# The last six units' second product: two token tiles by seven half-size products, and the order around it

## Chip, core and metric

The kernel runs on one core of a Trainium2 chip. The metric is the device time of one execution in microseconds (us); lower is better.

## What is computed

```python
def sm_attn(qq, kk, vv):
    s = scale * np.matmul(qq, kk.transpose(0, 1, 3, 2))
    a = np.exp(s - np.max(s, axis=-1, keepdims=True))
    a = a / (np.sum(a, axis=-1, keepdims=True) + 1e-09)
    return np.matmul(a, vv)
p_packed = sm_attn(p, k, v)            # p: (8, 8, 32, 64); k, v: (8, 8, 576, 64)
out = sm_attn(q, p_packed, p_packed)   # q: (8, 8, 576, 64)
x = out.transpose(0, 2, 1, 3).reshape(4608, 512)
xn = x / rms(x) * rms_g
return (silu(xn @ w_gate) * (xn @ w_val)) @ w_out    # 512 -> 1536 -> 512
```

8 batches of 8 heads, 576 tokens each, 32 packed rows per head. The three weights arrive as float64, all else as float32.

## The kernel before

**Products.** Since the second attention's output is a weighted sum of 32 packed rows, the kernel never forms x: it multiplies the packed rows of a batch into the gate and value weights once (packed weights, `packed_weights`: six chunks `c` of 256 columns for each of gate and value, kept in `ring`), and the attention weights `aTu` of the tokens are then the moving operand of the **first product** (line 1439). A float32 product is done in three float16 passes, high by high, high by low and low by high; each operand is therefore split into a high half (a cast) and a low half (a subtraction).

**Units.** The 4608 tokens are 12 units of 384, each three token tiles of 128. Units 1, 4, 7 and 10 hold tokens of two batches (192 columns of each). `mlp` runs the units: for each of 12 pieces `ft` of the hidden width six matmuls for gate and six for value (line 1439) into two PSUM rooms `pm`; `gated` makes silu(gate) * value (ScalarE, line 1520, and VectorE, line 1523), casts the high half into `hall` (ScalarE, line 1542) and subtracts for the low half (GpSimd, line 1545, or VectorE, line 1548). Then the **second product**: for each of three token tiles 12 x 3 matmuls of 512 columns (line 1506) into one PSUM room, from `hall` as the stationary operand and the split w_out, `wo`, as the moving one; in the last unit the third tile is done in two halves of 256 columns (line 1480). `store` evicts with the scale `invE` and sends the tile out.

**The start.** The gate and value weights arrive as 8-byte numbers in 12 pieces of 1 MB (`gv_piece`); `to_f32` makes float32 of the two words of each, with one conversion of a piece's low words on ScalarE (line 396) or GpSimd (line 391) or none but VectorE steps, as the string `LOW` says. For each chunk a Gram matrix of its columns (line 447), its largest entry (line 452) and a few one-column steps (lines 340 to 345, 460 to 467) give the powers of two by which the chunk is scaled. Packed weights of batches 0 to 2 use float32; from batch 3 on (`PW16_FROM`) a float16 copy, `wgv16`, made by `weights16` (lines 1072, 1074) in the same SBUF.

**Packed rows.** The first attention's values of a batch are made in two halves of heads, `pk`, by float32 matmuls (line 887), or, for batch 7 (`V16_FROM`), by float16 ones (line 809); each half is turned by a 64-row matmul (line 919).

**Order.** Every engine runs its instructions in order, and so does the queue of SyncE (SP), which issues nearly all transfers: loads, transposes (`DMA_TRANSPOSE`) and stores. The order comes from a list: each part of the kernel is a generator that asks for a PSUM or SBUF room (`Room`), for a mark of another part, or for an engine step, and `ORDER` names, step by step, which generator goes next. `FILLS` puts matmuls without a use (line 1603) at places of the start.

## Time and profile before

| | |
|---|---|
| time of three runs, us | 729.67 median (728.51 to 732.56) |
| the profiled execution, us | 728.67, its span 726.8 |
| TensorE busy | 708.9 us (98%), 8153 matmuls |
| VectorE, ScalarE, GpSimd busy | 465.2, 476.5, 213.4 us |
| chain of work that ended last | TensorE 83%, ScalarE 5%, DMA 4% |
| DMA | 86.73 MB moved, mean 119 GB/s |

The span runs from the first to the last instruction; the profiled execution's time is 1.9 us longer. Busy times of the engines overlap, so they don't add up; the chain is the sequence of steps in which each one waited for the one ahead of it.

### The profile page before, as it was taken

Reading aid. Unit: us, or ns where it says so; the run is one execution under the profiler, and the core shown is the slowest. Engines: PE = TensorE matmul, PEld = TensorE weight load, DVE = VectorE, ACT = ScalarE, POOL = GpSimd, SP = SyncE. Lnnn points to the kernel's source line nnn. Section 1 sums busy time; section 2 is a strip of 40 time slices with the busy share of each in tenths; the row PEclk is TensorE's granted clock in tenths of the full one; section 3 lists DMA queues with packets and bytes.
Section 4 is the critical chain, followed back from the end, with each engine's and each line's share of the span. In section 5 each row is a group of like instructions: output and inputs, shape, how many; then the busy total and the mean of one; then the engine's idle time right before and its main releaser. Section 6 shows DMA issues by size and latency. Waiting matters only on the chain.

```text
span 726.8 us, 19520 instructions
## 1 busy us (share of the span) xinstructions
PE 708.9 (98%) x8153; PEld 431.8 (59%) x8153; DVE 465.2 (64%) x1032; ACT 476.5 (66%) x982; POOL 213.4 (29%) x228
## 2 busy tenths in 40 slices
...
PEclk9999999999999999999999999999999999999999
...
GB/s 286 368 371 290 199 2 74 88 158 190 55 142 120 126 99 138 168 75 136 79 209 98 77 153 161 51 115 126 132 38 24 96 82 80 51 3 51 15 2 44
DMA packets 152923, 86.73 MB, mean 119 GB/s; under 512 B 116737, under 2 KB 140161, under 8 KB 152834
## 3 DMA queue, kind: packets, MB, share of 16 engines
...
q8 instruction: 64, 1.05, 0.6%
...
## 4 chain that ended last, share of the span: by engine, by line
PE 83%; ACT 5%; DMA 4%; SPq 3%; DVE 2%; issue 1%; POOL 1%; ACTq 0%; POOLq 0%; DVEq 0%
PE pm_2x L1439 10%; PE pm_0x L1506 10%; PE pm_1x L1439 9%; PE pm_3x L1439 9%; PE pm_1x L1506 9%; PE pm_3x L1506 9%; PE pm_0x L1439 8%; PE pm_2x L1506 5%; DMA hall<-in_moe_w_val_dram 2%; SPq L423 2%; PE psa L1238 2%; PE psb L887 1%; PE pm_1x L1052 1%; PE psa L756 1%; PE pm_0x L1052 1%
## 5 line engine op out<-in xcount | busy, mean ns | idle before, releaser
L1439 PEld LDWEIGHTS <-ring 128*128 128x128 f16 x2304 | 205.1, 98 | 83.8 <-issue 10.7
L1506 PEld LDWEIGHTS <-hall 128*128 128x128 f16 x1188 | 113.3, 98 | 137.1 <-issue 6.7
L1545 POOL TENSOR_TENSOR hall<-t_1x,hall 128x384 f16<-128x384 f32 x68 | 65.0, 956 | 229.9 <-ACT hall L1542 221.7
L1545 POOL TENSOR_TENSOR hall<-t_0x,hall 128x384 f16<-128x384 f32 x60 | 58.7, 978 | 124.0 <-ACT hall L1542 115.1
L1506 PE MATMUL pm_1x<-wo,hall 128*128 128x512 f16 x360 | 80.8, 379 | 1.3 <-issue 0.7
L1506 PE MATMUL pm_3x<-wo,hall 128*128 128x512 f16 x324 | 73.2, 379 | 0.0
L1506 PE MATMUL pm_0x<-wo,hall 128*128 128x512 f16 x324 | 72.6, 379 | 0.0
L1542 ACT CAST hall<-t_1x 128x384 f16<-128x384 f32 x69 | 35.0, 507 | 17.5 <-DVE t_1x L1523 17.3
L1439 PE MATMUL pm_2x<-aTu_0x,ring 128*128 128x384 f16 (+1 forms) x318 | 45.7, 287 | 0.0
L1542 ACT CAST hall<-t_0x 128x384 f16<-128x384 f32 x70 | 35.5, 507 | 15.1 <-DVE t_0x L1523 15.0
L1439 PE MATMUL pm_1x<-aTu_1x,ring 128*128 128x192 f16 (+1 forms) x318 | 44.7, 284 | 0.0
L1439 PE MATMUL pm_2x<-aTu_1x,ring 128*128 128x192 f16 (+1 forms) x324 | 44.7, 282 | 0.0
L1439 PE MATMUL pm_3x<-aTu_0x,ring 128*128 128x192 f16 (+1 forms) x306 | 42.4, 282 | 0.0
L1506 PE MATMUL pm_2x<-wo,hall 128*128 128x512 f16 x180 | 40.0, 379 | 0.0
L1439 PE MATMUL pm_3x<-aTu_1x,ring 128*128 128x192 f16 (+1 forms) x270 | 38.9, 287 | 0.2 <-ACT t_1x L1520 0.2
L1439 PE MATMUL pm_1x<-aTu_0x,ring 128*128 128x384 f16 (+1 forms) x246 | 38.8, 299 | 0.1
L1439 PE MATMUL pm_0x<-aTu_0x,ring 128*128 128x192 f16 (+1 forms) x282 | 38.0, 279 | 0.7 <-issue 0.7
L1439 PE MATMUL pm_0x<-aTu_1x,ring 128*128 128x384 f16 (+1 forms) x240 | 36.5, 294 | 0.0
L1074 POOL TENSOR_TENSOR wgv<-o_1x,wgv 128x512 f16<-128x512 f32 x20 | 23.4, 1172 | 41.3 <-ACT wgv L1072 41.1
L1520 ACT ACT_TABLE_LOAD x15 | 19.2, 1283 | 7.3 <-PE pm_1x L1439 2.4
L1520 ACT ACTIVATE t_0x<-pm_0x,usc_1x 128x384 f32<-128x384 f32 x13 | 7.5, 577 | 22.3 <-PE pm_0x L1439 21.6
L354 DVE SCALAR_TENSOR_TENSOR ring<-pm_1x,ring 128x512 f16<-128x512 f32 x17 | 11.7, 685 | 14.7 <-ACT ring L352 14.6
...
## 6 DMA issues: line engine op xcount, KB each, us to landing
...
hall<-in_moe_w_out_dram SPq DMA_DIRECT2D x4, 1024.0 KB, 6.1
...
wo<-in_moe_w_gate_dram SPq DMA_DIRECT2D x3, 1024.0 KB, 16.0
wo<-in_moe_w_val_dram SPq DMA_DIRECT2D x3, 1024.0 KB, 14.5
...
```

Of the source, the lines that this page charges most:

```text
L354: nc.vector.scalar_tensor_tensor(lo, x, s, hi, ALU.mult, ALU.subtract)
L423: nc.sync.dma_start(raw.rearrange("p k n e -> p k (n e)"), (w_gate, w_val)[n][:, 4 * c * P : 4 * (c + 1) * P].rearrange("(kt p) f -> p kt ...
L756: nc.tensor.matmul(psc[32 * j : 32 * j + 32, hf, : HC * CP], pT[:, 2 * g + hl, 32 * j : 32 * j + 32], kT[:, j * NCK + HC * hf : j * NCK + ...
L887: nc.tensor.matmul(pp[32 * j : 32 * j + 32, :D], a1T[:, c, 32 * j : 32 * j + 32], vf[:, j, cv, :], start=(c == 0), stop=(c == NCK - 1),)
L1052: nc.tensor.matmul(ps[e][32 * j : 32 * j + 32, :], pg[h, lp, j, :], wgv16[h, c, j, lw, :], start=(n3 == 0), stop=(n3 == 2),)
L1074: nc.gpsimd.tensor_tensor(wgv16[:, c, k, 1], st, wgv16[:, c, k, 0], ALU.subtract)
L1238: nc.tensor.matmul(ps2[o : o + n, i, :, pi, :], qT[:, lq, i, pi, o : o + n], packs[b][3][:, lp, pi, :, :], start=(j == 0), stop=(j == 2),)
L1439: nc.tensor.matmul(psi[:, :, o : o + n], pw[:, g, lw, w, f * P : (f + 1) * P], aT[:, :, la, g, o : o + n], start=(j == 0), stop=(j == 5),)
L1506: nc.tensor.matmul(po, hall[:, ft, lh, ts], wo[:, ft, 1 - lw, :], start=(n == 0), stop=(n == 3 * NFT - 1))
L1520: nc.scalar.activation(t, pss[0][:, :UT], AF.Silu, scale=sc[:, c, 0:1])
L1542: nc.scalar.copy(hall[:, ft, 0, :], t)
L1545: nc.gpsimd.tensor_tensor(hall[:, ft, 1, :], t, hall[:, ft, 0, :], ALU.subtract)
```

## The change

- **Units 6 to 11** (`STR_FROM`): tile 2 is done as before (line 1593 after the change). Tiles 0 and 1 are taken together with the two halves of the hidden width of each chunk and the two halves of the output as a 2 x 2 block product, done with seven products in place of eight: `seven`, 7 x 18 matmuls of 256 columns (line 1724). The sums of the four blocks of the left operand are made per chunk in `parts_of` (line 1678), by GpSimd for chunks 0, 2, 4 and VectorE for 1, 3, 5, then split (lines 1690); those of w_out once in `tees`; `together` adds the products from PSUM (line 1739).
- **Room** for these operands is what `wgv16` held: the float16 weights are written to DRAM (line 1165) and come back, 1 MB per chunk and batch, for batches 4 to 7 (`stream`, line 1105). Batch 7's values take the float32 path (`V16_FROM`).
- **Start**: `gram` is a part of its own and accumulates both column halves of a chunk in one place, so its reduction is 256 wide; some of its small steps and five byte conversions go to GpSimd.
- **Packed weights**: odd chunks from batch 2 on take the PSUM room `psc` in place of two `pm`. **Packed rows** of both halves of heads are turned by one matmul of 128 rows.
- A new `ORDER`, new `FILLS`, and scales that follow from the above.

```diff
-LOW = "DDPAAAPAPAPP"
+LOW = "DDPPPPPPPPPP"
...
-V16_FROM = 7
+V16_FROM = 8
+STREAM_FROM = 4
+STR_FROM = 6
+TEE_BY = "PPPPPP"
+SUM_BY = "PDPDPD"
+SLO_BY = "PPPPPP"
 KEYS_GATE = 'scored'
-PW_WIDE = 8
+PAIR_FROM = 2
...
+    dram = ctx.enter_context(tc.tile_pool(name="dram", bufs=1, space=bass.MemoryType.DRAM))
+    wdram = [dram.tile([P, NKT, 2, 512], F16, name=f"wdram{c}") for c in range(NFC)]
...
-        if n == 0:
-            return
-        yield ("w32", i - 1)
+    def gram(c):
         xb = wgv[:, c].bitcast(BF16)[..., 1::2]
+        yield ("w32", 2 * c)
         pn = yield Room("pa")
-        yield PE, pe(128, 16) + 0.24, plan.now, 1.0, 32
         for w in range(2):
-            for f in range(2):
-                for kt in range(NKT):
-                    r = xb[:, kt, w, f * P : (f + 1) * P]
-                    nc.tensor.matmul(
-                        pn[:, (2 * w + f) * P : (2 * w + f + 1) * P], r, r, start=(kt == 0), stop=(kt == NKT - 1)
-                    )
+            if w:
+                yield ("w32", 2 * c + 1)
+            yield PE, pe(128, 8) + 0.03, plan.now, 1.0, 16
+            for k in range(2 * NKT):
+                f, kt = divmod(k, NKT)
+                r = xb[:, kt, w, f * P : (f + 1) * P]
+                nc.tensor.matmul(pn[:, w * P : (w + 1) * P], r, r, start=(k == 0), stop=(k == 2 * NKT - 1))
         mx = tiny(2)
-        yield DVE, dve(512) + 0.04
-        nc.vector.tensor_reduce(mx, pn.rearrange("p (w f) -> p w f", w=2), AX.X, ALU.max)
+        yield DVE, dve(256) + 0.04
+        nc.vector.tensor_reduce(mx, pn[:, : 2 * P].rearrange("p (w f) -> p w f", w=2), AX.X, ALU.max)
         yield PE, pe(2, 2)
         nc.tensor.matmul(pn[:, 0:2], margin, upper(mx), start=True, stop=True)
+        u, s = tiny(2), gv_r[:, c]
+        yield DVE, 0.37
+        nc.vector.tensor_scalar(
+            u.bitcast(U32), pn[:, 0:2].bitcast(U32), 24, 23, ALU.logical_shift_right, ALU.logical_shift_left
+        )
+        nc.vector.tensor_single_scalar(s.bitcast(U32), u.bitcast(U32), EXP_MASK, ALU.bitwise_xor)
+        plan.give("pa", pn)
         yield "g",
-        yield DVE2, 0.82
-        u, s = tiny(2), gv_r[:, c]
-        norm_scale(u, s, pn[:, 0:2])
-        plan.give("pa", pn)
-        nc.vector.tensor_scalar(ratio[:, c : c + 1], u[:, 0:1], s[:, 1:2], 0.5, ALU.mult, ALU.mult)
-        t0 = plan.now
+        yield POOLS, 1.05
+        nc.gpsimd.tensor_scalar(u, u, 2.0**-126, 2.0**51, ALU.max, ALU.mult)
+        nc.gpsimd.tensor_scalar(s, s, 2.0**127, 2.0**-51, ALU.min, ALU.mult)
+        nc.gpsimd.tensor_scalar(ratio[:, c : c + 1], u[:, 0:1], s[:, 1:2], 0.5, ALU.mult, ALU.mult)
         plan.mark("pw_sc", c)
-        by = nc.gpsimd if GV_BY[c] == "P" else nc.vector
-        yield (POOLS, 2.0, t0) if GV_BY[c] == "P" else (DVE, 0.45, t0)
-        by.tensor_scalar(gv_sc[:, c, 0:1], u[:, 0:1], gmax, 2.0**-5, ALU.mult, ALU.mult)
-        by.tensor_scalar(gv_sc[:, c, 1:2], s[:, 0:1], gmax_r, 2.0**-12, ALU.mult, ALU.mult)
-        by.tensor_scalar(wo_sc[:, c : c + 1], u[:, 0:1], u[:, 1:2], gsq, ALU.mult, ALU.mult)
-        if H32:
-            by.tensor_scalar(gv_sc[:, c, 2:3], gv_sc[:, c, 1:2], wo_sc[:, c : c + 1], 2.0**-8, ALU.mult, ALU.mult)
+        yield POOLS, 1.05
+        nc.gpsimd.tensor_scalar(gv_sc[:, c, 0:1], u[:, 0:1], gmax, 2.0**-5, ALU.mult, ALU.mult)
+        nc.gpsimd.tensor_scalar(gv_sc[:, c, 1:2], s[:, 0:1], gmax_r, 2.0**-5, ALU.mult, ALU.mult)
+        nc.gpsimd.tensor_scalar(wo_sc[:, c : c + 1], u[:, 0:1], u[:, 1:2], gsq, ALU.mult, ALU.mult)
...
-        yield PE, pe(128, 8), t_p, 1.0, 8
-        for g in range(2):
-            nc.tensor.matmul(pt[64 * g : 64 * g + 64, : 4 * NPK], pks[g], ident32, start=True, stop=True)
+        yield PE, pe(128, 4), t_p, 1.0, 4
+        nc.tensor.matmul(pt[:, : 4 * NPK], pkp[0].rearrange("p g d -> p (g d)"), ident32, start=True, stop=True)
...
-            if b < PW_WIDE:
+            if b < PAIR_FROM or c % 2 == 0:
...
+            if b >= STREAM_FROM:
+                yield ("ws", b, c)
+                w16 = streamed.pop((b, c))
...
+    def stream():
+        for b in range(STREAM_FROM, B):
+            for c in range(NFC):
+                w16 = yield Room("wst")
+                yield ("dw", c)
+                yield LOAD, P * 8192
+                nc.sync.dma_start(w16, wdram[c])
+                streamed[b, c] = w16
+                plan.mark("ws", b, c)
...
+    def tees(i):
+        for c in range(2 + i // 2, NFC, NFC):
+            yield ("dw", c)
+            yield ("pwd", c)
+        yield ("wo_hl", i)
+        if i == 0:
+            a = yield Room("a1")
+            for k in range(2):
+                plan.give("t", a[:, UT * k : UT * (k + 1)])
+        o1 = yield Room("o")
+        o2 = yield Room("o")
+        by = nc.gpsimd if TEE_BY[i] == "P" else nc.vector
+        kind = (lambda n: (POOL, pool(n))) if TEE_BY[i] == "P" else (lambda n: (DVE2, dve(n)))
+        q = DM // 2
+        for x, f in ((o1, 2 * i), (o2, 2 * i + 1)):
+            yield kind(512)
+            by.tensor_tensor(x, wo[:, f, 1, :], wo[:, f, 0, :], ALU.add)
+        for a, b, d in ((o1[:, q:], o1[:, :q], o1[:, :q]), (o2[:, q:], o1[:, q:], o1[:, q:]), (o2[:, q:], o1[:, :q], o2[:, q:]), (o2[:, :q], o2[:, q:], o2[:, :q])):
+            yield kind(256)
+            by.tensor_tensor(d, a, b, ALU.subtract)
+        t0 = plan.now
+        for w, x in enumerate((o1, o2)):
+            yield ACT, act(512), t0
+            nc.scalar.copy(teev[:, i, w, 0], x)
+            yield DVE2, dve(512) + 0.08
+            nc.vector.tensor_tensor(teev[:, i, w, 1], x, teev[:, i, w, 0], ALU.subtract)
+            plan.give("o", x)
+        plan.mark("tee", i)
...
+            if k == NKT - 1:
+                yield LOAD, P * 8192
+                nc.sync.dma_start(wdram[c], wgv16[:, c])
+                plan.mark("dw", c)
...
-            for i in range(2 if u == 0 else 0, TPU):
+            for i in (2,) if u == 0 or u >= STR_FROM else range(TPU):
...
+            if u >= STR_FROM:
+                plan.add(together(u), "store", u, 0)
+                yield from seven(u)
...
+    def parts_of(u, ft, t, sc):
+        c, f = divmod(ft, 2)
+        x3 = t.rearrange("p (i n) -> p i n", i=TPU)
+        h3 = hall[:, ft].rearrange("p l (i n) -> p l i n", i=TPU)
+        own = slice(0, TPU) if f else slice(0, TPU, 2)
+        n = UT if f else 2 * P
+        yield ACT, act(n)
+        nc.scalar.copy(h3[:, 0, own], x3[:, own])
+        if (H_LO_MIXED if len(parts(u)) > 1 else H_LO_ONE)[ft] == "P":
+            yield POOL, pool(n)
+            nc.gpsimd.tensor_tensor(h3[:, 1, own], x3[:, own], h3[:, 0, own], ALU.subtract)
+        else:
+            yield DVE2, dve(n) + 0.08
+            nc.vector.tensor_tensor(h3[:, 1, own], x3[:, own], h3[:, 0, own], ALU.subtract)
+        plan.mark("h", u, ft)
+        if ft == NFT - 1:
+            plan.give("usc", sc)
+        if f == 0:
+            evens[c] = t
+            plan.mark("even", u, c)
+            return
+        yield ("even", u, c)
+        te = evens.pop(c)
+        a11, a21 = te[:, :P], te[:, P : 2 * P]
+        a12, a22 = t[:, :P], t[:, P : 2 * P]
+        x0 = yield Room("o")
+        x = x0.rearrange("p (k n) -> p k n", k=4)
+        by = nc.gpsimd if SUM_BY[c] == "P" else nc.vector
+        kind = (POOL, pool(P)) if SUM_BY[c] == "P" else (DVE2, dve(P))
+        for d, a, b, op in ((x[:, 0], a21, a22, ALU.add), (x[:, 1], x[:, 0], a11, ALU.subtract), (x[:, 2], a11, a21, ALU.subtract), (x[:, 3], a12, x[:, 1], ALU.subtract)):
+            yield kind
+            by.tensor_tensor(d, a, b, op)
+        t0 = plan.now
+        plan.give("t", te)
+        plan.give("t", t)
+        s12r = s12[:, c].rearrange("p l (k n) -> p l k n", k=2)
+        ends = []
+        for d, r in ((s12r, slice(0, 2)), (hall[:, 2 * c, :, P : 2 * P].unsqueeze(2), slice(2, 3)), (s4[:, c].unsqueeze(2), slice(3, 4))):
+            n = P * (r.stop - r.start)
+            yield ACT, act(n), t0
+            nc.scalar.copy(d[:, 0], x[:, r])
+            if SLO_BY[c] == "P":
+                yield POOL, pool(n)
+                nc.gpsimd.tensor_tensor(d[:, 1], x[:, r], d[:, 0], ALU.subtract)
+            else:
+                yield DVE2, dve(n) + 0.08
+                nc.vector.tensor_tensor(d[:, 1], x[:, r], d[:, 0], ALU.subtract)
+            ends.append(plan.now)
+        plan.now = max(ends)
+        plan.give("o", x0)
+        plan.mark("s", u, c)
...
+    def seven(u):
+        q = DM // 2
+        tile0, tile1 = slice(0, P), slice(P, 2 * P)
+        A = {
+            1: lambda c, l: hall[:, 2 * c, l, tile0], 2: lambda c, l: hall[:, 2 * c + 1, l, tile0],
+            3: lambda c, l: s4[:, c, l, :], 4: lambda c, l: hall[:, 2 * c + 1, l, tile1],
+            5: lambda c, l: s12[:, c, l, :P], 6: lambda c, l: s12[:, c, l, P:],
+            7: lambda c, l: hall[:, 2 * c, l, tile1],
+        }
+        w = lambda f, l, h: wo[:, f, 1 - l, q * h : q * (h + 1)]
+        W = {
+            1: lambda c, l: w(2 * c, l, 0), 2: lambda c, l: w(2 * c + 1, l, 0), 3: lambda c, l: w(2 * c + 1, l, 1),
+            4: lambda c, l: teev[:, c, 1, l, :q], 5: lambda c, l: teev[:, c, 0, l, :q],
+            6: lambda c, l: teev[:, c, 1, l, q:], 7: lambda c, l: teev[:, c, 0, l, q:],
+        }
+        for k in (1, 6, 7, 5, 2, 4, 3):
+            ps = yield Room("pm")
+            for c in range(NFC):
+                if c % 2 == 0:
+                    for d in (c, c + 1):
+                        yield ("h", u, 2 * d + 1)
+                        if k not in (1, 2, 4):
+                            yield ("s", u, d)
+                        yield ("tee", d)
+                    yield PE, pe(q, 6) + 0.006, None, 1.0, 12
+                for n3, (la, lw) in enumerate(((0, 0), (0, 1), (1, 0))):
+                    nc.tensor.matmul(
+                        ps[:, :q], A[k](c, la), W[k](c, lw), start=(c + n3 == 0), stop=(c == NFC - 1 and n3 == 2)
+                    )
+            products[u, k] = ps
+            plan.mark("p", u, k)
...
+    def together(u):
+        q = DM // 2
+        o1 = yield Room("o")
+        o2 = yield Room("o")
+        def take(k):
+            yield ("p", u, k)
+            return products.pop((u, k))
+        def add(d, ps, x):
+            yield DVE, dve(q) + 0.06
+            nc.vector.scalar_tensor_tensor(d, ps[:, :q], invE, x, ALU.mult, ALU.add)
+        dst = out[u * UT : (u + 1) * UT, :].rearrange("(p c) n -> c p n", c=TPU)
+        ps = yield from take(1)
+        yield ACT, act(q)
+        nc.scalar.activation(o1[:, :q], ps[:, :q], AF.Copy, scale=invE)
+        plan.give("pm", ps)
+        ps = yield from take(6)
+        yield from add(o2[:, q:], ps, o1[:, :q])
+        plan.give("pm", ps)
+        ps = yield from take(7)
+        yield from add(o2[:, :q], ps, o2[:, q:])
+        plan.give("pm", ps)
...
```

**VectorE in the start**, around one chunk's norm: `tensor_reduce` is the reduction of the Gram matrix, `tiny` and `gv_r` hold the powers of two, line 354 is the low half in an eviction of packed weights, line 413 a step of the weights' conversion to float32. Before:

```order
L452 TENSOR_REDUCE tiny_15x<-pm_1x 128x2
L354 SCALAR_TENSOR_TENSOR ring<-pm_0x,gv_r,ring 128x512
L340 TENSOR_SCALAR tiny_17x<-pm_1x 128x2
L344 TENSOR_SCALAR tiny_17x<-tiny_17x 128x2
L345 TENSOR_SCALAR gv_r<-tiny_17x 128x2
L460 TENSOR_SCALAR ratio<-tiny_17x,gv_r 128x1
L452 TENSOR_REDUCE tiny_16x<-pm_2x 128x2
L354 SCALAR_TENSOR_TENSOR ring<-pm_3x,gv_r,ring 128x512
```

After:

```order
L413 SCALAR_TENSOR_TENSOR wgv<-wgv,wo_78 128x4x256
L471 TENSOR_REDUCE tiny_13x<-pm_1x 128x2
L1215 TENSOR_SCALAR aT_0x<-psb 128x256
L476 TENSOR_SCALAR tiny_14x<-pm_1x 128x2
L479 TENSOR_SCALAR gv_r<-tiny_14x 128x2
L1009 SCALAR_TENSOR_TENSOR pg_0x<-pts_0x,sv_269,gcol 128x128
L471 TENSOR_REDUCE tiny_15x<-pm_3x 128x2
```

The reduction is followed by two small steps in place of four; the other evictions and steps between them are others now.

**GpSimd at the end of the last unit.** Before, one low half after another (`t_0x`, `t_1x` hold silu(gate) * value):

```order
L1545 TENSOR_TENSOR hall<-t_1x,hall 128x384
L1545 TENSOR_TENSOR hall<-t_0x,hall 128x384
L1545 TENSOR_TENSOR hall<-t_1x,hall 128x384
L1545 TENSOR_TENSOR hall<-t_0x,hall 128x384
L1545 TENSOR_TENSOR hall<-t_1x,hall 128x384
```

After, from the end of chunk 4 on (`wgv` and `misc` are the memory that now holds the sums' splits; line 1657 is the low half of line 1545, 2x128 where two of the three tiles need one):

```order
L1678 TENSOR_TENSOR wgv<-t_1x 128x128
L1678 TENSOR_TENSOR wgv<-t_0x,wgv 128x128
L1690 TENSOR_TENSOR wgv<-o_1x,wgv 128x256
L1657 TENSOR_TENSOR hall<-a_0x,hall 128x384
L1690 TENSOR_TENSOR wgv<-wgv 128x256
L1690 TENSOR_TENSOR hall<-o_1x,hall 128x128
L1690 TENSOR_TENSOR hall<-wgv,hall 128x128
L1690 TENSOR_TENSOR wgv<-o_0x,wgv 128x256
L1690 TENSOR_TENSOR misc<-o_1x,misc 128x128
L1690 TENSOR_TENSOR hall<-o_0x,hall 128x128
L1690 TENSOR_TENSOR misc<-wgv,misc 128x128
L1690 TENSOR_TENSOR misc<-o_0x,misc 128x128
```

Two sums of chunk 4 and its splits (256, 128, 128 columns), and those of chunk 5, stand among the low halves; chunk 5's sums are VectorE's.

**SyncE from the transposes of unit 8 to those of unit 9** (`aTu`). Before:

```order
L1396 DMA_TRANSPOSE aTu_0x<-hl_0x 128x12x128
L1206 DMA_TRANSPOSE big_3x<-big_4x 128x24x128
L1580 DMA out_dram<-o_1x 128x512
L799 DMA_TRANSPOSE a1T_0x<-hl_0x 128x12x128
L1156 DMA big_1x<-in_q_dram 64x8x192 x2
L1580 DMA out_dram<-o_0x 128x512
L1275 DMA_TRANSPOSE aT_0x<-hl_0x 128x12x128
L1580 DMA out_dram<-o_1x 128x512
L799 DMA_TRANSPOSE a1T_0x<-hl_0x 128x12x128
L1396 DMA_TRANSPOSE aTu_1x<-hl_0x 128x12x128
```

After, the last twelve rows up to the same place:

```order
L1765 DMA out_dram<-o_0x 128x512
L1775 DMA out_dram<-wgv 128x512
L570 DMA big_3x<-in_v_dram 96x4x384
L1804 DMA out_dram<-o_1x 128x512
L1105 DMA wgv<-wdram_134 128x4096
L1365 DMA_TRANSPOSE aT_0x<-hl_0x 128x12x128
L1105 DMA wgv<-wdram_135 128x4096
L1105 DMA wgv<-wdram_136 128x4096
L1246 DMA big_1x<-in_q_dram 64x8x192 x2
L880 DMA_TRANSPOSE a_1x<-hl_0x 128x12x128
L1105 DMA wgv<-wdram_131 128x4096
L1485 DMA_TRANSPOSE aTu_1x<-hl_0x 128x12x128
```

Reloads from `wdram` stand between stores, the transposes of `aT` and `a` and the load of q, ahead of the transpose of `aTu`.

## Rows read from the trace of the kernel before

**Rows 1.** The page: parts 1 and 2 (busy time; granted clock in 40 slices).

```profile
PE 708.9 (98%) x8153; PEld 431.8 (59%) x8153; DVE 465.2 (64%) x1032; ACT 476.5 (66%) x982; POOL 213.4 (29%) x228
PEclk9999999999999999999999999999999999999999
```

**Rows 2.** Windows: length, busy PE, PEld, DVE, ACT, POOL (count), clock, DMA share, GB/s.

```profile
0.00:58.79 58.79, 49.37 (x733) 37.73 (x734) 43.92 (x98) 40.85 (x71) 22.72 (x39) 1.00 1.02 347
20.00:40.00 20.00, 15.77 (x251) 13.12 (x250) 16.94 (x34) 14.65 (x22) 5.62 (x5) 1.00 1.05 384
40.00:60.00 20.00, 16.56 (x301) 12.07 (x289) 19.46 (x43) 19.48 (x39) 11.94 (x16) 1.00 1.05 379
160.00:180.00 20.00, 18.69 (x219) 9.01 (x219) 12.84 (x38) 12.79 (x31) 4.67 (x4) 1.00 0.87 177
220.00:240.00 20.00, 18.71 (x247) 8.84 (x246) 15.69 (x46) 10.69 (x25) 7.99 (x7) 1.00 0.71 128
483.00:543.00 60.00, 60.00 (x673) 35.30 (x671) 40.38 (x82) 42.34 (x86) 12.70 (x14) 1.00 0.52 115
```

**Rows 3.** The chain that ended last, from 690: start, length, what.

```profile
690.21 0.97 PE pm_2x L1439 x6
699.96 7.77 PE pm_0x L1506 x36
719.43 3.94 PE pm_3x L1480 x36
```

**Rows 4.** The same chain in mixed unit 1.

```profile
124.82 0.99 PE pm_2x L1439 x12
```

**Rows 5.** The page, part 5: two groups, busy us, mean ns of one.

```profile
L1439 PEld LDWEIGHTS <-ring 128*128 128x128 f16 x2304 | 205.1, 98 | 83.8 <-issue 10.7
L1545 POOL TENSOR_TENSOR hall<-t_1x,hall 128x384 f16<-128x384 f32 x68 | 65.0, 956 | 229.9 <-ACT hall L1542 221.7
```

**Rows 6.** Line 1545 on POOL: min/median/max ns; then who waited.

```profile
L1545 POOL TENSOR_TENSOR hall<-t_1x,hall x68: 904/914/1462, 67.1 to 701.7; 128x384 f16<-128x384 f32 x68
L1545 POOL TENSOR_TENSOR hall<-t_0x,hall x60: 910/914/1832, 69.5 to 699.4; 128x384 f16<-128x384 f32 x60
  ACT t_1x L1520: 4.3, 9
```

**Rows 7.** Other sizes on POOL, one on DVE (groups by shape); line 391.

```profile
L1074 POOL TENSOR_TENSOR wgv<-o_1x,wgv 128x512 f16<-128x512 f32 x20 | 23.4, 1172 | 41.3 <-ACT wgv L1072 41.1
L1023 POOL TENSOR_SCALAR pgh_0x<-pg_0x,ratio 128x128 f32<-128x128 f32 x2 | 1.2, 610 | 1.0 <-DVE ratio L460 1.0
L1023 DVE TENSOR_SCALAR pgh_0x<-pg_0x,ratio 128x128 f32<-128x128 f32 x2 | 0.6, 286 | 0.1
...
L391 POOL TENSOR_SCALAR hall<-hall x4: 1127/1440/1822, 40.5 to 75.8; 128x1024 uint32<-128x1024 uint8 x4
```

**Rows 8.** The start: lines 452 and 396, DVE groups before 62, the timeline at 57.

```profile
L452 DVE TENSOR_REDUCE tiny_15x<-pm_1x x1: 680/680/680, 42.1 to 42.1; 128x2 f32<-128x512 f32 x1
...
L396 ACT ACTIVATE wo<-wo x3: 1125/1136/1152, 30.7 to 44.2; 128x1024 uint32<-128x1024 uint8 x3
...
L1125 DVE TENSOR_SCALAR aT_0x<-psb 128x256 f32<-128x256 f32 x1 | 0.4, 411 | 0.0
L460 DVE TENSOR_SCALAR ratio<-tiny_18x,gv_r 128x1 f32<-128x1 f32 x1 | 0.2, 216 | 0.0
...
56.80 0.94 DVE L1138 SCALAR_TENSOR_TENSOR aTu_0x<-psa,aTu_0x 128x768 f16<-128x768 f32 x1
58.79 0.65 PE L1439 MATMUL pm_1x<-aTu_0x,ring 128*128 128x384 f16 x3
```

**Rows 9.** The page, part 6: a 1 MB load after the start, KB, us to landing.

```profile
hall<-in_moe_w_out_dram SPq DMA_DIRECT2D x4, 1024.0 KB, 6.1
```

**Rows 10.** Values of a batch half: line 809 in its stretch; line 887, timeline.

```profile
528.00:530.60 2.60, 0.76 (x72) 0.65 (x72) 1.00 0.00 0
...
87.05 0.88 PE L887 MATMUL psb<-big_1x,a1T_0x 96*32 96x64 f32 x48
```

229 lines of the change are left out of this document (151 added, 78 removed).

## The prediction

> **What bounds the kernel now.** I read the page first: TensorE (PE) is busy 708.9 us of the 726.8 us span, 98%, and its granted clock is full (2.4 GHz) in every slice [rows 1]. Whatever is to come out of the time must therefore be work taken from PE, or come out of the 17.9 us in which PE stands idle. The windows say where those lie: 9.42 us ahead of 58.79, where the first product of unit 0 begins, almost all of it from 20 to 58.79; a few gaps in the middle (1.31 and 1.29 us in the two stretches shown) and the last 3.4 us; from 483 to 543 PE has no gap at all [rows 2]. The chain of waits confirms it for the end: the last unit is matmul groups without a gap, 0.97 us for six of the first product, 7.77 us for a token tile of the second product, and 3.94 us for the last half tile, which ends at 723.37; behind it lie only its eviction and store [rows 3]. The other engines are far from full in the later units: in 60 us from 483 on VectorE (DVE) is busy 40, ScalarE (ACT) 42 and GpSimd (POOL) 13 [rows 2].
>
> **Change 1: seven products.** The chain prices both sides. A token tile of 36 matmuls of 512 columns takes 7.77 us, 215.8 ns each; 36 matmuls of 256 columns, each with its own weight load, take 3.94 us, 109.4 ns each [rows 3]. Two tiles are 72 x 215.8 = 15.54 us before; after, 7 products x 18 matmuls = 126 x 109.4 = 13.78 us, so 1.76 us less. In units 6 to 10 that is 5 x 1.76 = 8.8; in unit 11, where tile 2 was two halves of 3.94, the three tiles go from 7.77 + 7.77 + 7.88 = 23.42 to 7.77 + 13.78 = 21.55, 1.87 less. Together **-10.7 us**. The number that could spoil it is the weight load: 756 more loads stand ahead of half-size matmuls. A load takes 98 ns [rows 5], yet twelve 192-column matmuls with a load each take 0.99 us, 82.5 ns each [rows 4]: loads lie beside the matmuls even where they are longer, and the 109.4 ns were measured with a load each. I take them as hidden; unhidden they would cost 756 x 98 ns = 74 us.
>
> A rule of the Trainium skill speaks against the change: "TensorE: Matmul & The Clock Gate", section "Back-to-back issue gap", puts a sustained 512-column matmul at about 131 ns and a 128-column one at 81. By that, 72 x 131 = 9.4 us would become at least 126 x 81 = 10.2, and the change would lose. Six units of that would add some 5 us and the 10.7 would not come: about 734. This trace has 215.8 and 109.4 for these very shapes and line groups, so the sum goes by the trace, and the rule gets no more than the 0.01 of others below.
>
> **The price of it on the other engines.** Per unit POOL had twelve low halves of 384 columns, 0.914 us each [rows 6], 11 us less what DVE took. It now has six of 384, six of 256 (`parts_of`), twelve sums of 128 (chunks 0, 2, 4) and six times a low half of 256 and two of 128. No row has a tensor-tensor of 128 or 256 on POOL; 512 took 1.172 [rows 7] and 384 0.914, so 2.0 ns a column, and on that line 256 takes 0.66 and 128 0.40. The ends for 128: 0.305 (a third of 384) and 0.61 (the 128-column scalar multiply [rows 7]). I take the line, since it runs through two sizes of the same operation: 6 x 0.914 + 6 x 0.66 + 12 x 0.40 + 6 x (0.66 + 0.80) = 23.0 us a unit (ends 20 and 29). The first product of a unit is 12 x 2 x 0.97 = 23.3 us long, so POOL just keeps pace in it, and rests in the second product. What waits for it is the third pair of chunks (4 and 5) of product 6, first used 7.77 (tile 2) + 1.97 (product 1) + 1.31 = 11.05 us after the last first-product matmul. Before, the last low half began at 701.7 and so ended 2.65 us after that matmul (699.96) [rows 3, 6]; behind it come now four sums on DVE (0.286 each [rows 7]), a cast (0.35 or so, an estimate between these sums and the 0.41 of a 256-wide DVE operation [rows 8]) and three low halves, 1.46: 5.6 us. That leaves 5.4 us of cover: **0**. If POOL ran x times slower, 23.0x would reach past 23.3 + 5.4 from x = 1.25, and eat the whole 1.76 from x = 1.32. Line 1545's mean over its median is 956/914 = 1.05 [rows 5, 6].
>
> DVE gets twelve sums (3.4 us) and eight 256-column evictions (0.41 each, 3.3) for two 512-column ones a unit, ACT 18 more casts of 256 or 128 columns and six narrower ones; both have over 17 us idle in 60 [rows 2]: 0. Transforming w_out (`tees`, once: about 30 us of POOL by the same line, 12 casts and 12 subtractions of 512) is spread over units 5 and 6, with POOL at 13 of 60 there: 0.
>
> **Change 2: room.** The fp16 gate/value weights of batches 4 to 7 come back from DRAM, 24 MB read and 6 MB written, on the SP queue among the transposes and loads of the mixed units. A 1 MB load landed in 6.1 us [rows 9], and the queues are far from full there. But SP issues in order: a reload waits for one of two rooms, which the packed weights two chunks before give back, and transposes stand behind it. Batch 7's values go by the fp32 path: 72 small matmuls (0.76 us) become 48 of 0.88 us per half [rows 10]: 2 x 0.12 = **+0.2**; two more 768-wide additions go to POOL, far from its bound. New waits of PE in the middle: I take two as long as the two seen before, 1.31 + 1.29 = **+2.6**. Ends: -5.0 (all middle gaps of before close, 17.9 - 9.42 - 3.43, since odd chunks now have rooms of their own) and +18.3 (three landings of 6.1 in the open).
>
> **Change 3: the start.** From 40 to 60 DVE is busy 19.46 us and ACT 19.48 of 20, while PE has 3.44 us of gaps [rows 2]. The first product starts at 58.79, after DVE's `aTu` of 56.80 to 57.74 [rows 8]. Per chunk DVE loses half of a 512-wide reduction (0.68 to 0.41, the 256-wide price from PSUM) and two of four 0.2-us steps, 0.27 + 0.4 = 0.67; five of six chunks lie ahead: 3.3 us. ACT loses five conversions of 1.13 [rows 8], 5.7 us. Those go to POOL, with 11.94 of 20 in the same stretch. PE work ahead of the first product also changes (fewer fillers, packed weights and gram halves moved behind), but moved work saves nothing. I take DVE's share, **-3.3**, since DVE's chain is what the first product waits for. Ends: 0, because the DMA engines are at 1.05 there and may set the pace alone [rows 2], and -7.7, all of PE's gaps from 20 to 60.
>
> **Change 4: packed rows turned at once.** Two 64-row turns become one of 128, eight times: fp32 rows of the same 128 columns. At a few tenths of a us each at most, 0; this part saves nothing visible. The tail's one eviction in place of two and one 128 KB store in place of two of 64 KB: 0, within 0.9.
>
> **Sum.** 726.8 - 10.7 + 0.2 + 2.6 - 3.3 = 715.6; with the 1.9 us that lie around the span in the profiled execution (728.67) 717.5. The runs' median, 729.67, is 1.0 above that execution, so 717.5 to 718.5: **718 us**.
>
> **Rivals.**
> - *The start gains nothing* (DMA sets its pace): 718 + 3.3 = 721; with more gaps of the middle's kind up to 726. For it: DMA share 1.05 there. Against it: DVE and ACT saturated as well.
> - *The start gains all its gaps, or the middle closes*: 718 - 4.4 = 713.6, less 5.0 to 7.6 if the middle's go too: 706 to 713. Against it: a new order must place 30 more megabytes.
> - *POOL becomes the bound of units 6 to 11* (the other side). The place is the sums of chunk 5, ahead of product 6. For it: POOL's rows stretch beside a busy DVE, 1127 to 1822 ns for one operation at the start [rows 7], 914 to 1832 for line 1545, and ACT has waited for it (4.3 us) [rows 6]. At x = 1.4 a unit stalls 32.2 - 28.7 = 3.5 us, six of them 21: 739; at 1.6, 8.1 each: 767. It decides from x = 1.32. Against it: the mean factor is 1.05. The Trainium skill, "GPSIMD Engine Reference", sections "4.1 Engine selection" and "8. Key points", says that elementwise work is about twice as slow there as on VectorE and that the two contend for their SBUF interface. By this rule the sums belong elsewhere; the trace's stretched rows show such a mechanism, their median does not.
> - *The SP queue*: reloads hold transposes up in units 7 and 10. Three landings of 6.1 us: 718 - 2.6 + 18.3 = 734; one or two: 722 to 728.
> - *Weight loads not hidden*: 718 + 74 = 792.
>
> **How the numbers follow.** About 3.6 us (0.5% of 729.67) can be told from no change, so faster is below 726.0 and slower above 733.3. The forecast's case, 713 to 721.5: 0.54. Less than 713: 0.14. 721.5 to 726: 0.16. The queue: 0.09, two thirds of it within the bound. POOL: 0.05; loads: 0.01; 0.01 for others slower. Faster 0.84, same 0.06, slower 0.10. The range reaches from 709 to 727 and leaves out some 0.05 below and 0.14 above.
>
> **What would show it.** After: 756 matmuls of 256 columns at about 109 ns, in groups of 18 of 1.97 us without gaps; PE busy about 697; POOL busy about 330, its 128-column rows near 0.40; first product near 55.5; no wait of PE for POOL in units 6 to 11. I am wrong if products are over 2.1 us apart, if PE waits on `s12`, `s4` or casts behind POOL, if reloads hold transposes for microseconds, or if the first product starts no earlier than 58.

## The result

The changed kernel takes 723.63 us (median of ten runs, 722.16 to 728.26), the kernel before 730.14 in its runs beside it; the ratio is 0.9915, with an interval from 0.989 to 0.994. The forecast was 718, from 709 to 727.

The page of the profiled execution, parts 1, 3 and 6 (PE to be held against [rows 1], the load against [rows 9]):

```profile
PE 703.3 (97%) x8368; PEld 461.3 (64%) x8368; DVE 520.5 (72%) x1126; ACT 500.8 (69%) x1099; POOL 349.1 (48%) x468
...
HBM read 72.88 MB, written 15.73 MB: 122 GB/s over the span
...
wgv<-wdram SPq DMA_DIRECT2D x24, 1024.0 KB, 6.8
wdram<-wgv SPq DMA_DIRECT2D x6, 1024.0 KB, 4.5
```

PE has 8368 matmuls instead of 8153 and is busy less; POOL is busy 349 us instead of 213, and 25 MB more are read. This execution was the slowest of the ten, 728.26 us; where time is counted below, another one of the same kernel serves, 721.82 us with a span of 719.8 and the clock full throughout.

The chain of this profiled execution at the end of the last unit (start, length, what; [rows 3] are its counterpart):

```profile
701.46 7.77 PE pm_1x L1593 x36
709.23 1.97 PE pm_2x L1724 x18
...
721.02 1.98 PE pm_3x L1724 x18
...
723.03 0.48 DVE wgv L1739
```

The first product, tile 2 and the seven products stand without a gap, 1.97 us for 18 matmuls, and one eviction of 0.48 us follows. Tile 2 and seven products are 7.77 + 13.77 = 21.54 us; three tiles were 23.42.

Windows of that other execution (length, busy PE, PEld, DVE, ACT, POOL with counts, clock, DMA share, GB/s):

```profile
0.00:60.00 60.00, 53.87 (x728) 39.57 (x729) 44.51 (x90) 38.93 (x71) 34.60 (x56) 1.00 1.01 350
60.00:100.00 40.00, 37.65 (x456) 22.97 (x455) 35.57 (x74) 33.03 (x63) 21.04 (x25) 1.00 0.57 163
100.00:400.00 300.00, 295.02 (x3566) 175.81 (x3565) 234.25 (x515) 230.36 (x489) 133.45 (x128) 1.00 0.69 162
400.00:600.00 200.00, 196.23 (x2485) 134.07 (x2484) 149.22 (x328) 145.90 (x345) 105.04 (x165) 1.00 0.69 172
```

The same stretches of the kernel before, without the first:

```profile
60.00:100.00 40.00, 40.00 (x454) 25.43 (x453) 36.51 (x77) 34.51 (x64) 20.30 (x21) 1.00 0.57 165
100.00:400.00 300.00, 295.64 (x3574) 175.31 (x3572) 219.59 (x514) 225.74 (x482) 103.80 (x97) 1.00 0.58 119
400.00:600.00 200.00, 199.34 (x2387) 116.68 (x2386) 121.61 (x263) 130.52 (x274) 42.10 (x45) 1.00 0.45 96
```

From these, the ledger of the span, before against after (us):

| | forecast | measured | |
|---|---|---|---|
| PE busy | -10.5 | -9.8 | 708.9 to 699.1 |
| PE's gaps up to 100 us | -3.3 | -0.9 | 9.42 to 6.13 + 2.35 |
| PE's gaps from 100 to the last matmul | +2.6 | +3.9 | 5.05 to 8.90 |
| behind the last matmul | 0 | -0.1 | 3.43 to 3.31 |
| span | -11.2 | -7.0 | 726.8 to 719.8 |

The 8.90 is 719.8 - 699.1 less 8.48 and 3.31. In the profiled execution of the result the same gaps are 11.7 us (623.0 us less 611.3 of busy PE): executions of one kernel differ by almost 3 us there, and +3.9 is the low end. What the forecast missed by in this execution, 4.2 us, is 2.4 in the start, 1.3 in the middle and 0.7 of PE's busy time.

### The profile page after: what moved, and what is told of

The parts are those of the page before. It is cut to its first block, busy times and chain, and to the rows that moved or that the text cites. A ratio compares the mean times of both kernels' runs of the same rounds, so it can differ in the third digit from the quotient of the medians.

```text
span 726.3 us, 20459 instructions
## 1 busy us (share of the span) xinstructions
PE 703.3 (97%) x8368; PEld 461.3 (64%) x8368; DVE 520.5 (72%) x1126; ACT 500.8 (69%) x1099; POOL 349.1 (48%) x468
## 4 chain that ended last, share of the span: by engine, by line
PE 67%; ACT 8%; DMA 8%; DVE 8%; issue 4%; POOL 4%; SPq 1%; ACTq 0%; DVEq 0%; POOLq 0%
PE pm_2x L1528 7%; PE pm_3x L1528 7%; PE pm_0x L1528 7%; PE pm_1x L1528 7%; PE pm_2x L1593 5%; PE pm_1x L1593 4%; PE pm_3x L1593 4%; PE pm_0x L1593 3%; PE pm_2x L1724 3%; PE pm_3x L1724 3%; PE pm_1x L1724 2%; DMA aT_0x<-hl_0x 2%; PE pm_0x L1724 2%; PE psa L1328 1%; DMA big_2x<-in_v_dram 1%
## 5 line engine op out<-in xcount | busy, mean ns | idle before, releaser
L1593 PE MATMUL pm_1x<-wo,hall 128*128 128x512 f16 x252 | 56.6, 379 | 0.2 <-POOL hall L1638 0.2
L1638 POOL TENSOR_TENSOR hall<-t_0x,hall 128x384 f16<-128x384 f32 x29 | 29.6, 1021 | 51.0 <-ACT hall L1635 47.1
L1528 PE MATMUL pm_0x<-aTu_1x,ring 128*128 128x192 f16 (+1 forms) x306 | 44.4, 290 | 0.0
L1638 POOL TENSOR_TENSOR hall<-t_1x,hall 128x384 f16<-128x384 f32 x27 | 25.7, 952 | 37.0 <-ACT hall L1635 29.7
L1528 PE MATMUL pm_2x<-aTu_1x,ring 128*128 128x384 f16 (+1 forms) x276 | 40.0, 288 | 1.6 <-ACT t_1x L1610 0.9
L1593 PE MATMUL pm_3x<-wo,hall 128*128 128x512 f16 x180 | 41.3, 379 | 0.0
L1657 POOL TENSOR_TENSOR hall<-t_0x,hall 128x384 f16<-128x384 f32 x18 | 16.6, 923 | 44.3 <-ACT hall L1654 44.2
L1160 POOL TENSOR_TENSOR wgv<-o_0x,wgv 128x512 f16<-128x512 f32 x18 | 21.4, 1190 | 31.2 <-ACT wgv L1158 31.1
L1657 POOL TENSOR_TENSOR hall<-a_0x,hall 128x256 f16<-128x256 f32 (+1 forms) x32 | 26.7, 840 | 16.8 <-ACT hall L1654 16.7
L1593 PE MATMUL pm_0x<-wo,hall 128*128 128x512 f16 x144 | 32.2, 379 | 0.0
L885 POOL TENSOR_TENSOR a1T_0x<-a_1x 96x768 f32<-96x768 f16 x9 | 14.9, 1654 | 34.7 <-PE psa L1328 20.1
## 6 DMA issues: line engine op xcount, KB each, us to landing
wo<-in_moe_w_val_dram SPq DMA_DIRECT2D x3, 1024.0 KB, 11.1
```

The lines of the kernel that those rows point to most:

```text
L885: nc.gpsimd.tensor_tensor(a1T, x[:, 0], x[:, 1], ALU.add)
L1160: nc.gpsimd.tensor_tensor(wgv16[:, c, k, 1], st, wgv16[:, c, k, 0], ALU.subtract)
L1528: nc.tensor.matmul(psi[:, :, o : o + n], pw[:, g, lw, w, f * P : (f + 1) * P], aT[:, :, la, g, o : o + n], start=(j == 0), stop=(j == 5),)
L1593: nc.tensor.matmul(po, hall[:, ft, lh, ts], wo[:, ft, 1 - lw, :], start=(n == 0), stop=(n == 3 * NFT - 1))
L1638: nc.gpsimd.tensor_tensor(hall[:, ft, 1, :], t, hall[:, ft, 0, :], ALU.subtract)
L1657: nc.gpsimd.tensor_tensor(h3[:, 1, own], x3[:, own], h3[:, 0, own], ALU.subtract)
```

## The experiments

The reference for all of them is the changed kernel itself, 723.23 us. It ran on the same chip as three of them (the 512-column matmuls, the five conversions, the transfers of a sixteenth); the others ran on three more chips, where the kernel before took 729.3 to 729.7 us instead of 730.33. Held against the kernel before beside them, their differences shift by up to 1 us, so differences of that size say nothing. A trace is one execution each.

> The changed kernel itself, for comparison on one chip with the runs beside it, and for a trace of an execution whose clock is full throughout. Both theories: 722 to 725 us. The profiled execution behind the result had a granted clock of 0.92 and 0.91 in two 20-us stretches; with 1.00 throughout the span should be about 721 to 722 us.

Measured 723.23 us (721.82 to 723.91), span 719.8 at a clock of 1.00, as expected.

**An eighth product's work put back** (`seven`):

```diff
+                if c == 0 and k != 3:
+                    for la, lw in ((0, 0), (0, 1), (1, 0)):
+                        nc.tensor.matmul(ps[:, :q], A[k](c, la), W[k](c, lw), start=True, stop=True)
```

> The changed kernel with the work of an eighth product put back: six of the seven products are preceded by three more matmuls of 256 columns into the same room, which the product then overwrites; 18 a unit, no eviction added. Theory A (in units 6 to 11 PE's matmuls are the time, and the sums, splits and evictions lie beside them): 6 x 18 x 109.4 ns = 11.8 us slower than the changed kernel, 735. Theory B (something else has a share of the time there): less than 9 us. The run with 512-column matmuls in products 1 and 6 became 38.6 us slower instead of 13.8, because five products of one matmul each left five evictions of DVE in a row; here the pace of the evictions stays as it is, so theory A has to hold.

Measured 734.99 us, 11.8 more than the changed kernel, and slower than the kernel before (1.0071, from 1.0047 to 1.0095). The chain of its last unit, one extra piece and one product:

```profile
713.40 0.33 PE pm_2x L1725 x3
713.73 1.97 PE pm_2x L1727 x18
```

Every matmul added there is paid in full. That those saved were gained in full is argued from it, and fits the 10.7 us by which PE's busy time fell from 100 us on. All the rest of the change together, with eight products, would cost some 5 us against the kernel before.

**Tiles 0 and 1 by 512-column matmuls, the other five products one matmul each:**

```diff
+                if k not in (1, 6):
+                    if c == 0:
+                        nc.tensor.matmul(ps[:, :q], A[k](c, 0), W[k](c, 0), start=True, stop=True)
+                    continue
+                for f in (2 * c, 2 * c + 1):
+                    for n3, (la, lw) in enumerate(((0, 0), (0, 1), (1, 0))):
+                        nc.tensor.matmul(
+                            ps, hall[:, f, la, tile0 if k == 1 else tile1], wo[:, f, 1 - lw, :],
+                            start=(f + n3 == 0), stop=(f == NFT - 1 and n3 == 2),
+                        )
```

> The changed kernel, but in units 6 to 11 tiles 0 and 1 get 36 matmuls of 512 columns each (in the places of products 1 and 6), and the five other products are one matmul of 256 columns each; all sums, splits, reloads and evictions stay, so the output of these tiles is not the reference's. Theory A (PE is the bound there and everything else of the seven products is hidden): 6 x (72 x 215.8 + 5 x 109.4 - 126 x 109.4 ns) = 6 x 2.31 = 13.8 us slower than the changed kernel, about 737. Theory B (sums and splits cost something in the open): less than 11 us slower, because the longer products cover them.

Measured 761.87 us, 38.6 more; neither theory. The chain at the end of unit 10:

```profile
701.80 0.12 PE pm_0x L1725
701.92 0.48 DVE wgv L1745
...
704.60 2.08 PE pm_3x L1528 x6
706.68 1.64 PE pm_2x L1528 x6
708.32 0.97 PE pm_0x L1528 x6
```

With products of one matmul, the evictions of `together` have nothing to lie beside: from 701.80 to 704.60 PE waits for DVE, which holds the rooms. Then six matmuls of the first product take 2.08 and the next six 1.64 us instead of 0.97: the clock has fallen (0.83 from 700 to 710). So 2.8 + 1.8 + 2.3 us of matmuls are 6.9 a unit, 41 in six. The whole trace bears it out: 16.7 us more of gaps, and 23.0 more of busy PE, of which 13.8 are the matmuls. The experiment tells nothing of the sums; it tells that eight evictions a unit are hidden because a product of 1.97 us stands beside each. The eighth-product run, with the evictions' pace kept, replaces it.

**The block sums all on POOL, twice:**

```diff
-SUM_BY = "PDPDPD"
+SUM_BY = "PPPPPP"
...
             by.tensor_tensor(d, a, b, op)
+            by.tensor_tensor(d, a, b, op)
```

> The changed kernel with the block sums of all six chunks on GpSimd, each done twice: 48 sums a unit there instead of 12. With the 0.45 us that a sum takes in the trace, GpSimd's work is 12 x 0.45 = 5.4 + 18.2 = 23.6 us a unit in the changed kernel and 18.2 + 48 x 0.45 = 39.8 here. Theory A (the prediction's cover: 23.3 us of first product and 5.4 us behind it): a stall of about 39.8 - 28.7 = 11 us a unit, 67 us slower than the changed kernel, 790. Theory B (rooms for silu(gate) x value run out earlier, since they are given back behind the sums): the first product itself waits, more than 80 us slower. Theory C (GpSimd catches up in the second product's 21.5 us): under 40 us slower.

Measured 779.16 us, 55.9 more: between theories A (67) and C (under 40). From the page, and two kinds of PE's waits from 420 us on (waiter <- awaited: us, times, longest):

```profile
PE 717.4 (92%) x8368; PEld 464.2 (60%) x8368; DVE 498.7 (64%) x1054; ACT 502.5 (65%) x1099; POOL 446.9 (58%) x684
...
PE pm_0x L1528 <- ACT a_0x L1610: 5.9, 2, 3.3
PE pm_3x L1725 <- POOL wgv L1691: 5.6, 3, 2.8
```

PE waits in the seven products, for the splits on POOL, and in the first product and tile 2, for ACT's silu, which has no room for its result as long as POOL has not given one back: ahead of line 1610 ScalarE was idle for 33.5 us until a sum on POOL ended, as theory B has it. From 420 us on PE's gaps are 46.4 us, against 7.2 in the changed kernel: 39.2 more, 6.5 a unit. Most of the rest is PE's busy time, 717.4 us instead of 699.1 for the same 8368 matmuls, at a granted clock of 0.91 to 1.00 in stretches of 60 us. So 39.8 - 6.5 makes the cover 33.3 us; predicted were 28.7.

**The block sums all on POOL, once:**

```diff
-SUM_BY = "PDPDPD"
+SUM_BY = "PPPPPP"
```

> The changed kernel with the block sums of all six chunks on GpSimd, once each: 24 sums of 0.45 us a unit there, 18.2 + 10.8 = 29.0 us of GpSimd work a unit in place of 23.6. With twice as many sums (39.8 us) the kernel became 55.9 us slower than the changed one, 9.3 us a unit. Theory A (cover of 28.7 us, as predicted): 0.3 us a unit, so within 2 us of the changed kernel, with no wait for GpSimd in the products or a few tenths. Theory B (GpSimd has less cover, some 24 us, as the rooms behind the sums run out first): 4 to 5 us a unit, 25 to 30 us slower. By a straight line from the doubled run, 39.8 - 9.3, the cover would be 30.5, and the time unchanged.

Measured 723.06 us, 0.2 less than the changed kernel: theory A. Its only wait of PE from 420 us on that belongs to the seven products is 0.2 us for ScalarE's eviction of a product (line 1743).

**Five conversions back to ACT:**

```diff
-LOW = "DDPPPPPPPPPP"
+LOW = "DDPAAAPAPAPP"
```

> The changed kernel with the string LOW as before: five conversions of 1.13 us go back from GpSimd to ScalarE. Theory A (the prediction's: the start waits for DVE's chain, and ACT's relief adds nothing): within 1 us of the changed kernel. Theory B (ACT's relief of 5.7 us carries part of the start): 2 to 5 us slower, with new gaps of PE before 60 us that end with ACT.

Measured 726.22 us, 3.0 more: within theory B. PE's timeline, the pieces behind its two longest new gaps (start, length, what, idle before and what ended it):

```profile
29.58 1.03 PE L468 MATMUL pm_1x<-wgv 128*128 128x128 bf16 x8 [1.81 <-DVE wgv L418]
...
51.52 0.63 PE L468 MATMUL psb<-wgv 128*128 128x128 bf16 x8 [1.80 <-DVE wgv L418]
```

Both end with line 418, DVE's join behind an ACT conversion. By 100 us this execution's PE has 9.27 us of gaps against 8.48, 0.8 more, and its granted clock in the first 60 us is 0.97 where it was 1.00. From 100 to 600 us its gaps are 11.1 us against 8.75; a wait for the load of v is 0.7 longer there (2.44 against 1.74). That the move off ACT helps is shown by the runs, 723.14 to 727.86 us against 721.82 to 723.91 on one chip; how much of the 3.0 is gaps of the start, later gaps or the clock is not.

**DVE given its work back** (`gram`: the reduction twice, the exclusive-or three times):

```diff
+        nc.vector.tensor_reduce(mx, pn[:, : 2 * P].rearrange("p (w f) -> p w f", w=2), AX.X, ALU.max)
...
+        for _ in range(2):
+            nc.vector.tensor_single_scalar(s.bitcast(U32), u.bitcast(U32), EXP_MASK, ALU.bitwise_xor)
```

> The changed kernel, with DVE given back what the new gram chain took from it: per chunk the 256-wide reduction (0.42 us) and two more of the small exclusive-or steps (0.17 us each), results unchanged, 0.76 us for each of six chunks. Theory A (the start is paced by DVE): 2.5 to 4.5 us slower than the changed kernel. Theory B (the 3.3 us of gaps that went before 60 us went because of ACT, or of the order): within 1 us. If A holds before 60 us but PE's gaps from 60 to 100 shrink by as much, DVE's work up to 100 us is the bound, not its work up to the first product.

Measured 726.60 us, 3.4 more: theory A. Its windows:

```profile
0.00:60.00 60.00, 49.95 (x700) 36.38 (x701) 45.59 (x101) 36.76 (x65) 30.76 (x54) 1.00 1.01 348
60.00:100.00 40.00, 38.20 (x471) 24.45 (x468) 36.59 (x76) 32.39 (x62) 21.91 (x28) 1.00 0.59 165
```

Of the 4.6 us more of DVE, five chunks of six, 3.8 us, lie before 60 us. They make 3.9 us more of gaps there (10.05 against 6.13), of which 0.55 comes back from 60 to 100.

**DVE relieved behind the first product** (five joins of w_out on 16 columns; `at` is 0 only for w_out):

```diff
-            nc.vector.scalar_tensor_tensor(d, d, 3, lo, ALU.logical_shift_left, ALU.bitwise_or)
+            w = slice(0, 8) if at == 0 else slice(None)
+            nc.vector.scalar_tensor_tensor(d[..., w], d[..., w], 3, lo[..., w], ALU.logical_shift_left, ALU.bitwise_or)
```

> The changed kernel with five DVE steps of w_out's conversion, 1.22 us each between 58 and 77 us, cut from 1024 columns to 16, so that DVE has about 5 us less there and no other engine more; w_out's low words are then not joined on. The kernel with 4.6 us more on DVE ahead of the first product became 3.4 us slower. Theory A (DVE's work up to about 90 us sets when PE is through with the start, so relief behind the first product counts as well): PE's gaps from 60 to 100, 2.35 us, lose 1.2 us or more and the time falls by 1 to 3 us, to 720 to 722. Theory B (the gaps from 60 to 100 come from ACT or from the order of the steps): within 0.7 us of the changed kernel, and the gaps stay.

Measured 721.69 us, 1.5 less (719.17 to 726.87, a wide spread). Against the kernel before beside it that is 0.9892, from 0.9848 to 0.9936; the changed kernel's 0.9907 lies inside, so the time shows no gain. Its windows:

```profile
0.00:60.00 60.00, 53.99 (x728) 39.78 (x729) 43.32 (x90) 39.10 (x71) 34.63 (x58) 1.00 1.01 351
60.00:100.00 40.00, 38.90 (x467) 24.19 (x465) 32.93 (x78) 34.57 (x64) 17.57 (x25) 1.00 0.59 161
```

The gaps from 60 to 100 fall from 2.35 to 1.10 us, those before 60 stay: by the gaps theory A, which the time doesn't confirm. The waits that ended with DVE are gone; the two that are left, 0.69 and 0.41 us, end with ACT.

**POOL relieved, no other engine loaded** (its fifteen conversions on 8 columns):

```diff
-            nc.gpsimd.tensor_scalar(lo, lo.bitcast(U8)[..., 3::4], 1 / 32, -15.5 / 32, ALU.mult, ALU.add)
+            nc.gpsimd.tensor_scalar(lo[:, 0, :8], lo.bitcast(U8)[..., 3::4][:, 0, :8], 1 / 32, -15.5 / 32, ALU.mult, ALU.add)
...
-            nc.vector.scalar_tensor_tensor(d, d, 3, lo, ALU.logical_shift_left, ALU.bitwise_or)
+            nc.vector.scalar_tensor_tensor(d, d, 3, lo, ALU.logical_shift_left, ALU.bitwise_and)
```

> The changed kernel with the fifteen conversions of low words on GpSimd cut from 1024 columns to 8, so that GpSimd has some 13 us less in the first 80 us and no other engine more. The low words are then not converted, and the weights are other numbers. Theory A (GpSimd's conversions hold up DVE's steps, and their landing sets DVE's pace): PE's gaps before 100 us, 8.5 us, lose 2 us or more, and the kernel gains as much. Theory B (the stretching costs nothing, since DVE's own work is the bound): within 1 us of the changed kernel.

Measured 722.58 us, 0.65 less, inside the spread of either. Its windows:

```profile
0.00:60.00 60.00, 54.80 (x740) 40.99 (x740) 42.83 (x92) 39.51 (x72) 21.14 (x58) 1.00 1.01 352
60.00:100.00 40.00, 38.48 (x455) 23.47 (x453) 35.14 (x76) 33.91 (x63) 15.01 (x24) 1.00 0.57 161
```

The gaps up to 100 us are 6.72 instead of 8.48, 1.8 less, somewhat short of theory A's 2. At its wait near 88 us for line 963 PE is 1.8 us earlier than in the changed kernel, 86.55 against 88.37; but from 100 to 600 us its gaps are 9.8 us against 8.75, and the time doesn't show the gain. Between the theories, and left there.

**Two steps of that stretch on other engines:**

```diff
-LOW_WO = "PPPDPP"
+LOW_WO = "PPADPP"
...
-H_LO = "DPPPPPPDPPPP"
+H_LO = "PPPPPPPDPPPP"
```

> The changed kernel with two steps of the stretch from 60 to 70 us on other engines: one conversion of w_out from GpSimd to ScalarE (it took 2.13 us on GpSimd beside a step of DVE that took 0.90 instead of 0.17), and the low half of the first piece of unit 0 from DVE (1.29 us beside GpSimd, 0.55 alone) to GpSimd. Output unchanged. Theory A (DVE and GpSimd hold each other up there, and DVE paces unit 0): PE's gaps from 60 to 100, 2.35 us, lose 1 us or more, and the time 1 to 2 us. Theory B (ACT, 33 of 40 us busy there, is the bound): no change, or up to 1 us slower, with the gaps behind ACT longer.

Measured 723.05 us, no change, and the gaps from 60 to 100 are 2.11 us: theory B, for an edit that relieves DVE by about one step.

**Reloads and writes of a sixteenth:**

```diff
-                nc.sync.dma_start(w16, wdram[c])
+                nc.sync.dma_start(w16[:, 0, 0, :256], wdram[c][:, 0, 0, :256])
...
-                nc.sync.dma_start(wdram[c], wgv16[:, c])
+                nc.sync.dma_start(wdram[c][:, 0, 0, :256], wgv16[:, c, 0, 0, :256])
```

> The changed kernel, but each write and each reload of a weight chunk moves only a sixteenth of it (64 KB instead of 1 MB); the issues, their order and their waits stay. The packed weights of batches 4 to 7 are then made from other data. Theory A (the 30 MB crowd the transposes and loads of the middle): the gaps behind the load of v (1.63 us) and the transpose aT (1.65 us) go, those behind ACT in units 4 and 7 shrink, and it is 4 to 6 us faster than the changed kernel, 718 to 720. Theory B (the middle gaps come from ACT, DVE and the new order): within 1 us of the changed kernel, and the gaps behind ACT and DVE stay. In between, 1.5 to 3.5 us, both have a share.

Measured 720.14 us, 3.1 less: in between. PE's waits of the changed kernel from 100 to 600 us, the four largest kinds:

```profile
PE pm_2x L1528 <- ACT t_1x L1610: 2.0, 3, 0.9
PE psb L916 <- DMA big_1x<-in_v_dram: 1.7, 1, 1.7
PE psa L1087 <- ACT a_1x L797: 0.9, 1, 0.9
PE psa L1408 <- DMA aT_0x<-hl_0x: 0.9, 1, 0.9
```

and the windows without the bytes:

```profile
100.00:400.00 300.00, 296.44 (x3574) 176.43 (x3573) 235.84 (x521) 232.21 (x493) 133.53 (x128) 1.00 0.58 121
400.00:600.00 200.00, 196.43 (x2486) 134.16 (x2484) 147.62 (x322) 145.69 (x349) 106.98 (x168) 1.00 0.47 101
```

The wait for v shrinks from 1.74 to 0.54 us, and the transpose of aT no longer keeps PE waiting, though 0.47 us for DVE (line 374) stand in its place; the gaps from 100 to 600 fall from 8.75 to 7.13, 1.6 us, and a wait of 0.3 us near 397 is gone. Those behind ACT and DVE, 0.8 to 1.0 each in units 4 and 7, stay as they are. By these two executions the bytes are about 1.6 us of the 3.9 that came to the middle; the median's 3.1 also holds that these runs lie closer together (719.49 to 721.31).

**Three transfers later in the order:**

```diff
-L1165 DMA wdram_134<-wgv 128x4096
...
 L570 DMA big_1x<-in_v_dram 96x4x384
-L1105 DMA wgv<-wdram_131 128x4096
+L1165 DMA wdram_134<-wgv 128x4096
...
+L1105 DMA wgv<-wdram_131 128x4096
...
-L1105 DMA wgv<-wdram_135 128x4096
 L1365 DMA_TRANSPOSE aT_0x<-hl_0x 128x12x128
 L669 DMA_TRANSPOSE big_2x<-big_4x 128x24x96
+L1105 DMA wgv<-wdram_135 128x4096
```

> The changed kernel with three transfers later in the order: the write of the fourth weight chunk behind the load of batch 4's v, the first reload behind the next two loads and a store, and one reload of batch 6 behind the transpose of aT and the one after it. Nothing else changes, and the output is the reference's. Theory A (these three transfers make the v load and the transpose aT late, 1.74 and 0.88 us of gap in the trace): 1 to 3 us faster than the changed kernel, 720 to 722. Theory B (late for other reasons, or the reloads are now late themselves): no change or slower, with a gap behind the reload.

Measured 732.00 us, 8.8 more: theory B, and worse than it. The longest wait of PE from 400 to 500 us:

```profile
PE pm_2x L1087 <- DMA wgv<-wdram: 5.9, 1, 5.9
```

The reload that was put behind two transposes is now what packed weights wait for, 5.9 us, and from 486 to 492 us the granted clock is 0.50. The other end did no good either: v's wait went from 1.74 to 0.24, but the next one, behind ACT, grew from 0.29 to 2.34. The three were moved at once, so the 8.8 is not split between them. The SP queue has little slack at these places: with the reload ahead of the transpose PE waited 0.9 us for the transpose, with two transposes ahead of the reload 5.9 for the reload.

## Why the prediction was right, and where its sizes were off

The seven products gave what was forecast, and the range holds the time. The forecast's own case, 713 to 721.5 us, did not come: 723.63 lies where the prediction, with a chance of 0.16, put its rival that the start gains nothing.

**Seven products, -10.7: right.** 1.97 us a product and 7.77 for tile 2 stand in the chain as worked out, and the eighth product costs 11.8. PE's busy time fell by 9.8 instead of 10.5. By stretch it rose by 0.9 up to 100 us (90.6 to 91.5) and fell by 10.7 from there to the last matmul (618.3 to 607.6); which work moved across 100 us was not followed up.

**The price on the other engines, 0: right.** A sum of 128 columns takes 0.45 us on POOL (forecast 0.40), a low half of 256 columns 0.67 and of 128 0.43 (0.66, 0.40); POOL is busy 347.5 us in all, forecast about 330. Lines 1678 and 1690, min/median/max ns:

```profile
L1678 DVE TENSOR_TENSOR o_1x<-a_0x x9: 277/281/511, 426.5 to 692.6; 128x128 f32<-128x128 f32 x9
L1678 POOL TENSOR_TENSOR o_1x<-t_1x,t_0x x4: 448/454/633, 471.1 to 677.7; 128x128 f32<-128x128 f32 x4
...
L1690 POOL TENSOR_TENSOR wgv<-o_1x,wgv x12: 659/673/870, 432.8 to 697.1; 128x256 f16<-128x256 f32 x12
L1690 POOL TENSOR_TENSOR hall<-o_1x,hall x12: 417/426/470, 434.1 to 699.4; 128x128 f16<-128x128 f32 x12
```

In that execution units 6 to 11 have no wait for POOL. With 29.0 us of POOL work a unit nothing is lost, and by the waits with 39.8 us the cover is 33.3, where 28.7 was worked out. The rival that ends slower needed a stretching of 1.3; the medians of the groups shown are within 3% of their minima, though a single sum took up to 1.18 us. "GPSIMD Engine Reference" of the Trainium skill, section "4.1 Engine selection", has POOL about twice as slow as VectorE in such work; here a sum takes 0.45 against 0.28, 1.6 times. The rule holds in kind and would have been a reason to leave the sums on DVE; in a stretch where PE sets the time it decides nothing.

**The start, -3.3: the term that was mis-sized, -0.9.** The step read "I take DVE's share, -3.3, since DVE's chain is what the first product waits for". Before 60 us the gaps did fall by 3.3 (9.42 to 6.13), but that this is the forecast's number is luck: the new order also starts the first product at 49.1 us instead of 58.79, earlier than the 55.5 forecast, so the stretch holds other work. PE then waits in unit 0, where it had not waited at all: 2.35 us from 60 to 100. Its waits there (us, times, longest):

```profile
PE pm_1x L1528 <- ACT a1T_0x L868: 0.8, 1, 0.8
PE pm_1x L1528 <- DVE ring L374: 0.6, 1, 0.6
PE pm_3x L1528 <- ACT pts_0x L963: 0.4, 1, 0.4
PE pm_0x L1528 <- DVE t_0x L1613: 0.4, 1, 0.4
```

The two that end with DVE lie before 72 us, and DVE is busy 11.88 of the 12 us from 60 to 72; the two that end with ACT come after. DVE's busy time up to 100 us fell by only 1.6 us, 81.6 to 80.1. The two experiments on DVE show the step's error: work added ahead of the first product costs PE time nearly one for one, and less work behind it takes away the two waits that end with DVE (in the gaps of one execution; the time doesn't show it). So DVE paces PE up to about 72 us and the first product is no boundary; what remains behind it is ACT's, which the step left out. A relief of a saturated engine should be counted up to the point where it is no longer saturated. The reason that the rival gave, that the DMA engines alone set the pace, is not what the runs show: before 60 us the gaps fell by 3.3 with the DMA share at 1.02 before and 1.01 after, and grew by 3.9 with work on DVE at 1.01.

**New waits, +2.6: +3.9 in the trace.** That the two are near each other is partly luck. The forecast kept the old gaps and added two as long; in the trace nearly all the old ones are gone, first of all (waiter <- awaited: us, times, longest)

```profile
PE psb L887 <- POOL a1T_0x L861: 2.7, 2, 1.4
```

Of 5.05 us, 2.7 were these two. The 8.90 us that stand there now are other gaps: 2.8 end with transfers, nearly all the rest with ACT or DVE. The rival of the SP queue is a part of it: without the reloads' bytes 1.6 us of gaps go in the trace, 3.1 us in the runs' medians. The waits behind ACT and DVE, most of them in the mixed units 4 and 7, stay without the bytes; what in the order makes them was not tried.

**Weight loads:** PEld is busy 460 us instead of 432, and the half-size matmuls keep 109 ns each with a load ahead of every one: hidden, as taken. The prediction's 756 more loads were miscounted, though the sum doesn't use them: 5 x (126 - 72) + (162 - 144) = 288 more matmuls, each with its load, stand in the second products of units 6 to 11, so in the open they would cost 28 us, not 74. "TensorE: Matmul & The Clock Gate" of the Trainium skill, section "Back-to-back issue gap", has about 131 ns for a sustained matmul of 512 columns and 81 for 128; by the prediction's estimate from them the change would have been a loss. Tile 2's 36 still take 7.77 us, 215.8 each, so this kernel doesn't show that rate, and the measurement decides.
